# Mixing over the sequence on column quarters and row quarters of the PE array

## The chip, the cores and the metric

The kernel runs on one core of a Trainium2 chip. Its time is device microseconds (us) of one execution; lower is better. Three executions of the kernel before were timed, and a fourth was recorded by the hardware profiler. The engines are PE (matrix multiply, with PEld for its weight loads), DVE (vector), ACT (scalar), POOL (GpSimd) and SP, which issues the DMAs.

## What is computed

The inputs are q, k and v for 4 batches of 8 heads, 576 tokens, 64 wide, all float32, and the matrices U (576 x 32), V (32 x 576), w_ch1 (512 x 2048) and w_ch2 (2048 x 512), which arrive as 64-bit floats.

```python
q_rot, k_rot = (rotate(q), rotate(k))            # rotary embedding
scores = scale * np.matmul(q_rot, k_rot.transpose(0, 1, 3, 2))
scores = scores - np.max(scores, axis=-1, keepdims=True)
attn = np.exp(scores)
attn = attn / (np.sum(attn, axis=-1, keepdims=True) + 1e-09)
x = np.matmul(attn, v)                           # then as (batch, 576, 512)
h = x.transpose(0, 2, 1) @ U @ V                 # the mix over the sequence
u = x + h.transpose(0, 2, 1)
ch = np.maximum(u @ w_ch1, 0.0) @ w_ch2
out = u + ch
```

## The kernel before

**Stages.** Attention of a batch runs over four head pairs (`hp`, 128 features each) and, within a pair, over five token tiles (`t`): four of 128 tokens and a rest of 64 (`REM`). A tile's scores go into the PSUM buffers `s`, DVE finds the maximum (`junk`, `nb`), ACT takes the exponential (`p`), ACT and POOL split it into two f16 halves, and SP turns them by a transposing DMA (`pt<-p`). PE multiplies by V in f16 parts (`pv`), the result is divided by the row sums into `xf` (tokens on partitions), and PE turns that against an identity (`ident`) into `x` (features on partitions). The scores of batches 0 and 1 are f32 matmuls of 64 rows, two heads on the two row halves of the array; batches 2 and 3 use three f16 matmuls instead.

**The mix** (`mix`, line 1123) follows each second head pair, so twice a batch. `project` multiplies `uf` by the five `xf` tiles of two pairs: 5 f32 matmuls of 256 columns into one PSUM bank. `uf` (filled in `prep_uv`, line 643) holds U three times side by side and a fourth block of zeros, so 96 of the 128 result rows carry the same product. `parts` copies them into `gt` as f32r, a reduced-precision 4-byte type, and DVE writes what was rounded off into rows 32 to 63. `spread` then multiplies `gt` by `vst` (V three times, one copy holding V's own rounding rest): per chunk of 128 features 2 f32r matmuls of 288 columns. DVE adds the result to `x` and takes the largest magnitude, `am`.

**Scales.** `pow2_scale` and `half_scales` add a per-partition sum over the 128 partitions by a matmul with an all-ones matrix (`ones`, f32, 1 or 2 columns) and make a power of two of it. This happens 21 times in all: once per batch for V and for u (4 + 4), for the five weight groups, and for eight head pairs of batches 2 and 3.

**The MLP** works on 8 halves (batch, 288 tokens). The first half of batch 0 is plain f32 (`mm<-x,wt` and an f32 form of `mm<-room,wt`, 256 matmul records); the other seven take three f16 matmuls of 288 columns per product (`mm<-u,wt`, `mm<-room,wt`, 2,688 records). Attention of batch b+1 is interleaved with the MLP of batch b. A half can start when `ready[b]` has the scale of u, which needs the whole mix of its batch.

**What sets the order.** The class `Plan` records every step with its engine and its reads and writes, gives each a cost (`cost`, `transfer`, `lag`), places them as early as their engine and inputs allow, and orders each engine by the start times. Then each row of `MOVES` (52 of them: a seed, a spread, a begin and a width) shakes a stretch of that order; the shortest by the planner's own costs is kept and emitted. The engines' queues follow it strictly. All instructions therefore carry line 379 in the profile, and are told apart by their tiles.

Of the kernel before, what the change touches and what calls it, by code (L numbers as in the profile page):

```python
# [59 lines left out]
class Plan:  # L60
# [85 lines left out]
    @staticmethod  # L146
    def cost(calls):

        us = 0
        for eng, op, a, k in calls:  # L150
            out = k.get("out", a[0] if a else None)
            ins = [k[i] for i in ("in_", "in0", "in1") if i in k]
            n = max(free(x) for x in [out] + ins)
            by = sum(hasattr(k.get(i), "tensor") for i in ("scale", "scalar", "scalar1", "scalar2"))
            psum = any(x.space == PSUM for x in ins)
            if eng == "tensor":
                m = free(a[1] if op == "transpose" else a[2])
                if op == "transpose":
                    us += free(a[0]) / 1200
                    if "xf" in a[1].tensor.name:  # L160
                        us += 0.05 if free(a[0]) > 64 else 0.12
                elif a[2].dtype == F32:

                    k = 2 if list(a[1].ap)[0][1] <= 64 and m > 256 and len(calls) == 4 else 1
                    us += max(m * 4, 640 if free(a[1]) > 1 and m > 1 else 256) / 2400 / k
                    us += 0.05 * (k > 1)
                else:
                    k = 2 if list(a[1].ap)[0][1] <= 64 and len(calls) == 12 else 1
                    us += max(m, 64) * (4 if a[2].dtype == F32R and m < 256 else 1) / 2400 / k
                us += 0.003  # L170
            elif eng == "vector":
                fast = op in ("tensor_scalar", "tensor_copy") and not psum
                us += n * (0.00052 if fast else 0.00104)
                us += 0.008 if op == "memset" else 0.069 + 0.062 * by
            elif eng == "scalar":
                by += "accum_out" in k
                by += hasattr(k.get("bias"), "tensor")
                us += n * 0.00083 + (0.053 if psum else 0.094) + 0.093 * by
            elif op == "memset":
                us += 0.035 + n * 0.00083  # L180
            elif op == "tensor_tensor":
                us += 0.148 + n * (0.0021 if k["in1"].dtype in (F32, F32R) else 0.00189)
            else:
                us += 0.161 + 0.083 * by + n * 0.00083
        eng, op, a, k = calls[0]
        if eng == "tensor" and op == "matmul":
            if list(a[1].ap)[0][1] <= 64 and len(calls) in (4, 12):
                us += 0.18 if len(calls) == 12 else 0.06
            elif len(calls) == 5 and free(a[2]) == 256:
                us += 0.3  # L190
            elif a[2].dtype == F32R:
                us += 0.07
            elif free(a[2]) <= 2:
                us += 0.12
        return us
# [36 lines left out]
    def transfer(calls):  # L232
# [3 lines left out]
        if op == "dma_start_transpose":  # L236
            return 1.37, 0.9, 1.3, 0.98
# [3 lines left out]
        return hw, hw + 0.65, rows * free(sb) * SIZE[sb.dtype] / 360e3, 1.2  # L241
# [36 lines left out]
    def lag(a, b, turn=False):  # L278

        if a == "sync":  # L280
            return 0.98 if turn else 1.2
# [121 lines left out]
def tile_rope_attention_then_mixer(ctx, tc, qk, v, tab, u_in, v_in, w1, w2, out):  # L403
# [54 lines left out]
    ones = cst.tile([P, P], F32, name="ones")  # L458
# [30 lines left out]
    vst = cst.tile([P, S], F32R, name="vst")  # L489

    uf = cst.tile([P, NC, 4 * R], F32, name="uf")
    xfs = [cst.tile([P, 2, P], F32, name=f"xf{t}") for t in range(NC)]
# [32 lines left out]
    gt = cst.tile([P, DM], F32R, name="gt")  # L525
# [58 lines left out]

    def pow2_scale(sq, nm, up):
# [3 lines left out]
        nc.tensor.matmul(pb[:, 0:1], ones, sq, start=True, stop=True)  # L589
# [53 lines left out]
    def prep_uv():  # L643
# [10 lines left out]
        room = u.rearrange("p a c s -> p (a c s)").bitcast(F32)  # L654
        vr = room[:, 0:S]
        ur = room[:, S:S + NC * R].rearrange("p (c r) -> p c r", r=R)
        single((ur[:, 0:NT], ud[:, 0:NT]), (ur[0:REM, NT], ud[0:REM, NT]), (vr, vd))
        fill(uf[:, :, 3 * R:4 * R], 0.0)
        for n, cc in ((P, slice(0, NT)), (REM, slice(NT, NC))):
            for i in range(3):  # L660
                copy(uf[:n, cc, i * R:(i + 1) * R], ur[:n, cc, :], "ADP")
        copy(vst, vr, "ADP")
        lo = slice(2 * R, 3 * R)
        two(vst[lo, :], vr[lo, :], vst[lo, :].bitcast(F32), ALU.subtract, "DP")


# [222 lines left out]
    def half_scales(b, hp):  # L889
# [8 lines left out]
        nc.tensor.matmul(pb[:, 0:2], ones, sq, start=True, stop=True)  # L898
# [149 lines left out]
    def values(b, hp, t, pts, sm):  # L1048
# [25 lines left out]
        def evac():  # L1074
# [10 lines left out]
            xt = xfs[t][:, hp % 2]  # L1085
# [19 lines left out]
        def turn():  # L1105
# [7 lines left out]
            nc.tensor.transpose(tp[:, 0:n], xt[0:n], ident[0:n, 0:n])  # L1113
# [6 lines left out]
        if hp % 2 and t == NT:  # L1120
            mix(b, hp // 2)

    def mix(b, i):

        x, am = state[b]["x"], state[b]["am"]
        hold = {}

        beside = b == 0 and i < BES

        def project():  # L1130
            hold["t1"] = bank("") if beside else scores(1)[:, 0]
            with nc.group():
                for t in range(NC):
                    n = P if t < NT else REM
                    nc.tensor.matmul(
                        hold["t1"][:, 0:256], uf[:n, t, :],
                        xfs[t][:n].rearrange("p c d -> p (c d)"),
                        start=(t == 0), stop=(t == NT),
                    )

        def parts():
            g = gt[:, i * 256:(i + 1) * 256]
            t1 = hold["t1"]
            copy(g, t1[:, 0:256], "AD")
            lo = slice(R, 2 * R)
            nc.vector.tensor_tensor(
                out=g[lo, :], in0=t1[lo, 0:256], in1=g[lo, :].bitcast(F32), op=ALU.subtract
            )

        def spread(c):  # L1150
            xc = x[:, c, :].rearrange("p (n s) -> p n s", n=2)
            ph = None if beside else scores(1)
            for n in range(2):
                o = bank("") if beside else ph[:, n]
                nc.tensor.matmul(
                    o[:, 0:HS], gt[:, c * P:(c + 1) * P], vst[:, n * HS:(n + 1) * HS],
                    start=True, stop=True,
                )
                if beside:
                    nc.vector.tensor_tensor(  # L1160
                        out=xc[:, n], in0=o[:, 0:HS], in1=xc[:, n], op=ALU.add
                    )
            if not beside:
                nc.vector.tensor_tensor(out=xc, in0=ph[:, :, 0:HS], in1=xc, op=ALU.add)
            nc.vector.tensor_reduce(
                out=am[:, c:c + 1], in_=x[:, c, :], axis=AX.X, op=ALU.max,
# [3 lines left out]
        def last():  # L1170
            am1 = tmp("amu1", [1], 2, f"amu1{b}")
            nc.vector.tensor_reduce(out=am1, in_=am, axis=AX.X, op=ALU.max)
            sq = tmp("squ", [1], 2, f"squ{b}")
            nc.vector.tensor_tensor(out=sq, in0=am1, in1=am1, op=ALU.mult)


            ready[b] = (x, *pow2_scale(sq, f"u{b}", 4))

        project()
        parts()  # L1180
        spread(2 * i)
        spread(2 * i + 1)
        if i == NP // 2 - 1:
            last()
# [7 lines left out]
    def open_batch(b):  # L1192
        state[b].update(
            am=tmp("amu", [NP], 2, f"amu{b}"),
# [306 lines left out]
```

## Time and profile before

| | us |
|---|---|
| three timed executions | 678.32, 679.35, 679.36 (median 679.35) |
| the profiled execution, span from first to last instruction | 671.3 |
| what lies around the span (median less span) | 8.05 |
| PE busy / DVE / ACT / POOL, of the span | 620.9 / 437.1 / 388.1 / 239.1 |

The profiled execution's time is its span and the 8.05 us around it. A PE record is one pass: an f32 matmul has two records. Matmuls are pipelined, so the duration of one record is longer than its share of PE's time; what a row of matmuls costs is read from its start to the start of the next row.

### The profile page before, as it was taken

To read this page: it belongs to the slowest core of one execution; us is meant where nothing else is said; L and a number is where in the kernel's file an instruction comes from. 1 tells how busy PE (TensorE), PEld (TensorE's weight loads), DVE (VectorE), ACT (ScalarE), POOL (GpSimd) and SP (SyncE) were. 2 spreads that over 40 slices of the span, in tenths; PEclk is the share of its full clock that TensorE was granted. 3 is DMA by queue.
4 is the path that set the end of the run, shared out by engine and by line. 5 is a ranking of instruction groups with operands and counts; after the bars stand their busy time and mean duration, and the time that the engine had idled before them with its cause. 6 is when DMAs were issued, how large, how long until landed. Compare 5 with 4: busy or idle time off the path is not lost.

```text
span 671.3 us, 15150 instructions
## 1 busy us (share of the span) xinstructions
PE 620.9 (92%) x5914; PEld 467.9 (70%) x5914; DVE 437.1 (65%) x1096; ACT 388.1 (58%) x794; POOL 239.1 (36%) x205
## 2 busy tenths in 40 slices
PE   2677887999998999999999999999999999999998
PEld 1445555777776677777777777777777777777776
DVE  4678887999877866767767775667768643430310
ACT  3647775576877687467765874468766661320210
POOL 1456653013366567033454543044433450000000
PEclk9978888999999999999999999999999999999999
DMA  8899999979968657346786768168564561000000
GB/s 245 177 262 226 233 213 277 354 227 214 185 125 178 139 96 124 105 129 127 144 140 132 141 116 159 40 155 174 106 132 84 102 118 46 19 1 27 10 10 27
DMA packets 198056, 92.57 MB, mean 138 GB/s; under 512 B 173280, under 2 KB 186592, under 8 KB 197984
## 3 DMA queue, kind: packets, MB, share of 16 engines
q1 hardware_dynamic: 197984, 91.61, 61.6%
q8 instruction: 46, 0.75, 0.5%
q14 instruction: 26, 0.21, 0.1%
HBM read 41.70 MB, written 4.72 MB: 69 GB/s over the span
## 4 chain that ended last, share of the span: by engine, by line
PE 50%; DMA 7%; DVE 3%; issue 2%; ACT 2%; POOL 2%; SPq 0%; ACTq 0%; POOLq 0%; DVEq 0%
PE mm L379 38%; PE s L379 7%; DMA pt<-p 5%; PE pv L379 5%; DMA raw<-qk 1%; ACT p L379 1%; POOL p L379 1%; DVE junk L379 1%; DVE room L379 0%; DVE raw L379 0%; DVE u L379 0%; POOL raw L379 0%; ACT room L379 0%; SPq L379 0%; DVE x L379 0%
## 5 line engine op out<-in xcount | busy, mean ns | idle before, releaser
L379 PEld LDWEIGHTS <-wt 128*128 128x128 f16 x2688 | 255.0, 98 | 73.4 <-issue 13.2
L379 POOL TENSOR_TENSOR p<-p,p 128x576 f16<-128x576 f32 x130 | 171.6, 1328 | 209.3 <-ACT p L379 144.7
L379 PE MATMUL mm<-room,wt 128*128 128x288 f16 (+1 forms) x1472 | 219.6, 297 | 0.0
L379 PE MATMUL mm<-u,wt 128*128 128x288 f16 x1344 | 183.6, 286 | 1.7 <-DVE room L379 1.4
L379 ACT ACTIVATE room<-mm 128x288 f16<-128x288 f32 (+1 forms) x128 | 52.0, 408 | 97.1 <-PE mm L379 90.1
L379 PE MATMUL s<-qk,qk 64*128 64x288 f16 (+1 forms) x640 | 84.7, 371 | 18.8 <-DVE qk L379 11.2
L379 PEld LDWEIGHTS <-pt 128*128 128x128 f16 x1918 | 79.0, 100 | 29.6 <-DMA pt<-p 16.6
L379 DVE SCALAR_TENSOR_TENSOR room<-mm,room 128x288 f16<-128x288 f32 x112 | 50.9, 456 | 67.8 <-ACT room L379 67.2
L379 ACT ACTIVATE p<-p 128x576 f16<-128x576 f32 x130 | 86.9, 681 | 12.1 <-DMA pt<-p 10.6
L379 DVE TENSOR_SCALAR_CACHE_REDUCE junk<-s,bqk 128x576 bf16<-128x576 f32 x72 | 58.1, 812 | 22.7 <-PE s L379 18.6
L379 ACT ACTIVATE p<-s,nb,bqk 128x576 f32<-128x576 f32 x72 | 59.0, 828 | 21.6 <-DVE nb L379 14.9
L379 ACT ACTIVATE p<-s,nb 128x576 f32<-128x576 f32 x72 | 51.9, 737 | 26.0 <-DVE junk L379 20.3
L379 DVE TENSOR_SCALAR_CACHE_REDUCE junk<-s 128x576 bf16<-128x576 f32 x72 | 52.6, 753 | 18.4 <-PE s L379 16.6
L379 PE MATMUL pv<-vh,pt 128*128 128x65 f16 (+1 forms) x600 | 57.4, 200 | 6.7 <-DMA pt<-p 5.6
L379 PE MATMUL pv<-vl,pt 128*128 128x64 f16 (+1 forms) x600 | 57.2, 200 | 0.3 <-DVE vl L379 0.3
L379 PEld LDWEIGHTS s<-qk,qk 64*128 64x128 f32 x256 | 30.2, 216 | 33.0 <-ACT p L379 13.0
L379 DVE SCALAR_TENSOR_TENSOR ob<-mm,so,x 128x288 f32<-128x288 f32 x28 | 14.4, 514 | 41.3 <-PE mm L379 41.2
L379 ACT ACTIVATE xf<-pv,rc 128x64 f32<-128x64 f32 (+1 forms) x95 | 25.7, 309 | 25.6 <-DVE rc L379 23.0
L379 PE MATMUL pv<-vb,pt 128*128 128x65 f16 (+1 forms) x480 | 36.5, 200 | 1.1 <-DMA vb<-vh 1.1
L379 PE MATMUL mm<-x,wt 128*128 128x288 f32 x128 | 33.9, 420 | 1.7 <-DVE x L379 1.6
L379 DVE TENSOR_SCALAR rs<-pv,sc_v 128x2 f32<-128x2 f32 x67 | 14.5, 217 | 29.8 <-PE pv L379 28.5
L379 ACT ACTIVATE x<-mm 128x128 f32<-128x128 f32 (+1 forms) x59 | 15.5, 263 | 30.7 <-PE mm L379 30.5
(148 smaller groups left out, 714.9 us busy)
## 6 DMA issues: line engine op xcount, KB each, us to landing
raw<-qk SPq DMA_DIRECT2D x30, 576.0 KB, 4.6
wt<-w SPq DMA_DIRECT2D x23, 512.0 KB, 5.8
out_t<-ob SPq DMA_DIRECT2D x32, 144.0 KB, 2.0
raw<-vt SPq DMA_DIRECT2D x8, 512.0 KB, 4.8
x<-w SPq DMA_DIRECT2D x6, 512.0 KB, 5.5
vb<-vh SPq DMA_DIRECT2D x8, 264.0 KB, 4.9
pt<-p SPq DMA_TRANSPOSE x130, 3.3
u<-w SPq DMA_DIRECT2D x3, 512.0 KB, 5.4
```

The source lines that it names most:

```text
L379: getattr(getattr(nc, eng), op)(*a, **k)
```

## The change

Three things are altered in the computation.

- **Mix.** `uf` holds U once (32 columns) in f32 and `vst` holds V four times, unsplit. Per token tile and chunk one f32 matmul of 128 columns gives 32 result rows; chunk c writes to partitions 32c to 32c+31 of one bank, so the four chunks use the four column quarters of the array. The copy into `gt` is f32 and has no rounding rest. The spread takes chunk c from rows 32c to 32c+31: f32 matmuls of 32 rows and 288 columns on four row quarters, into four PSUM banks. Batch 0 still mixes after each second pair, on two quarters; batches 1 to 3 mix once, after the last pair, and there the spread goes in two rounds, one for each half of the sequence, which reuse the two `s` buffers.
- **Last token tile.** Rows 64 to 127 of its `xf` and `uf` are zero, so its turn and its projection use all 128 rows.
- **Scales.** `ones` and the summed column are bf16 (the upper half of each f32), one pass instead of two.

Several of the planner's costs are altered, and `MOVES` has 169 rows instead of 52, all with other numbers; the whole order is made anew.

```diff
 MOVES = (
-    (2201, 0.3, -489, 100), (7090, 0.3, -200, 40), (3748, 0.3, -65, 10), (365, 0.3, -230, 10),
...
+    (8915, 3, -514, 40), (390, 0.3, -332, 20), (5639, 0.3, -292, 40), (9035, 0.3, -270, 100),
...
-    ones = cst.tile([P, P], F32, name="ones")
+    ones = cst.tile([P, P], BF16, name="ones")
...
-    vst = cst.tile([P, S], F32R, name="vst")
-    uf = cst.tile([P, NC, 4 * R], F32, name="uf")
-    xfs = [cst.tile([P, 2, P], F32, name=f"xf{t}") for t in range(NC)]
+    vst = cst.tile([P, S], F32, name="vst")
+    uf = cst.tile([P, NC, R], F32, name="uf")
+    xfs = [cst.tile([P, NP, P], F32, name=f"xf{t}") for t in range(NC)]
...
+    def upper(sq):
+        return sq.bitcast(BF16)[:, 1::2]
...
-        nc.tensor.matmul(pb[:, 0:1], ones, sq, start=True, stop=True)
+        nc.tensor.matmul(pb[:, 0:1], ones, upper(sq), start=True, stop=True)
...
-        fill(uf[:, :, 3 * R:4 * R], 0.0)
-        for n, cc in ((P, slice(0, NT)), (REM, slice(NT, NC))):
-            for i in range(3):
-                copy(uf[:n, cc, i * R:(i + 1) * R], ur[:n, cc, :], "ADP")
-        copy(vst, vr, "ADP")
-        lo = slice(2 * R, 3 * R)
-        two(vst[lo, :], vr[lo, :], vst[lo, :].bitcast(F32), ALU.subtract, "DP")
+        fill(uf[REM:P, NT, :], 0.0)
+        fill(xfs[NT][REM:P], 0.0)
+        single((uf[:, 0:NT], ud[:, 0:NT]), (uf[0:REM, NT], ud[0:REM, NT]), (vst, vd))
...
-            nc.tensor.transpose(tp[:, 0:n], xt[0:n], ident[0:n, 0:n])
+            nc.tensor.transpose(tp[:, 0:P], xt, ident)
...
-                    nc.tensor.matmul(
-                        hold["t1"][:, 0:256], uf[:n, t, :],
-                        xfs[t][:n].rearrange("p c d -> p (c d)"),
-                        start=(t == 0), stop=(t == NT),
+                for c in cc:
+                    nc.tensor.matmul(
+                        t1[own[c]], uf[:, t], xfs[t][:, c], start=t == 0, stop=t == NT
                     )
...
+        def spread(ways):
+            with nc.group():
+                for o, c, n in ways:
+                    nc.tensor.matmul(
+                        o[:, 0:HS], gt[own[c]], vst[own[c], n * HS:(n + 1) * HS],
+                        start=True, stop=True,
+                    )
+
+        if len(cc) == NP:
+            for n in range(2):
+                hs = slice(n * HS, (n + 1) * HS)
+                ph = [scores(b) for _ in range(NP // 2)]
+                spread([(ph[c // 2][:, c % 2], c, n) for c in cc])
+                for i, p in enumerate(ph):
+                    xc = x[:, 2 * i:2 * i + 2, hs]
+                    nc.vector.tensor_tensor(out=xc, in0=p[:, :, 0:HS], in1=xc, op=ALU.add)
+                    largest(2 * i, 2, hs, 2 * n + 4 * i)
```

The order shows the mix of batch 1 on PE. Before, the second of its two projections (`xf_85` to `xf_89` are the five token tiles, `uf` is U, `s_62` the result, `wt` the MLP's weights) stands among MLP matmuls:

```order
L379 LDWEIGHTS wt
L379 MATMUL mm_65<-u,wt 128x288
L379 MATMUL s_62<-xf_85,uf 128x256
L379 MATMUL s_62<-xf_86,uf 128x256
L379 MATMUL s_62<-xf_87,uf 128x256
L379 MATMUL s_62<-xf_88,uf 128x256
L379 MATMUL s_62<-xf_89,uf 128x256
```

The one projection of batch 1 after the change, with its neighbours on PE:

```order
L414 LDWEIGHTS wt
L414 MATMUL mm_64<-room,wt 128x288
L414 MATMUL mm_66<-xf_85,uf 32x128 x4
L414 MATMUL mm_66<-xf_86,uf 32x128 x4
L414 MATMUL mm_66<-xf_87,uf 32x128 x4
L414 MATMUL mm_66<-xf_88,uf 32x128 x4
L414 MATMUL mm_66<-xf_89,uf 32x128 x4
```

Two rows of five matmuls with 256 columns became one row of twenty with 128 columns and 32 result rows, and the result moved from an `s` buffer to a bank.

On DVE, the end of batch 1's mix before (`gt` is the projection, `x_72` the activations, `amu` the largest magnitudes, `squ` the input of the scale of u):

```order
L379 TENSOR_TENSOR raw_100<-raw_100 128x576
L379 TENSOR_TENSOR gt<-s_61,gt 32x256
L379 TENSOR_TENSOR x_72<-s_61,x_72 128x576
L379 TENSOR_TENSOR x_72<-s_62,x_72 128x576
L379 TENSOR_REDUCE amu<-x_72 128x1 x2
L379 TENSOR_REDUCE amv_130<-amv 128x1
L379 TENSOR_REDUCE amu_136<-amu 128x1
L379 TENSOR_TENSOR squ<-amu_136 128x1
```

and the same place on DVE after the change:

```order
L414 TENSOR_TENSOR raw_100<-raw_100 128x576
L414 TENSOR_TENSOR x_72<-s_61,x_72 128x2x288
L414 TENSOR_TENSOR x_72<-s_62,x_72 128x2x288
L414 TENSOR_REDUCE amu<-x_72 128x2 x2
L414 TENSOR_REDUCE amv_130<-amv 128x1
L414 TENSOR_TENSOR x_72<-s_62,x_72 128x2x288
L414 TENSOR_TENSOR x_72<-s_61,x_72 128x2x288
L414 TENSOR_REDUCE amu<-x_72 128x2 x2
L414 TENSOR_REDUCE amu_136<-amu 128x1
L414 TENSOR_TENSOR squ<-amu_136 128x1
```

The subtraction for `gt` is gone, and the adds and reductions of the first two chunks, which stood some eighty instructions earlier, now stand at the batch's end with the others. On PE 15 MLP matmuls stand between the two rounds of this spread, and 30 between its last matmul and the sum for `squ` in batch 3; 21 MLP matmuls of batch 2 follow that sum, before and after the change.

On SP, the DMA issues of batch 0's third head pair before (`wt<-w` loads 512 KB of MLP weights):

```order
L379 DMA_TRANSPOSE pt<-p_2_98 128x9x128
L379 DMA wt<-w 128x2x512
L379 DMA_TRANSPOSE pt<-room 128x9x128
L379 DMA_TRANSPOSE room<-room 128x9x128
L379 DMA_TRANSPOSE pt<-p_0_96 128x9x128
```

and, after the change, the longest row of such loads on SP in batch 0:

```order
L414 DMA_TRANSPOSE pt<-room 128x9x128
L414 DMA_TRANSPOSE room<-room 128x9x128
L414 DMA wt<-w 128x2x512 x6
L414 DMA_TRANSPOSE pt<-p_0_96 128x9x128
L414 DMA_TRANSPOSE pt<-p_1_97 128x9x128
```

Loads that stood one or two at a time between the transposes stand six in a row, and about as many have been issued by the end of that stretch.

## Rows read from the trace of the kernel before

**Rows 1.** The page's span, and its busy time of the engines.
```profile
span 671.3 us, 15150 instructions
...
PE 620.9 (92%) x5914; PEld 467.9 (70%) x5914; DVE 437.1 (65%) x1096; ACT 388.1 (58%) x794; POOL 239.1 (36%) x205
```

**Rows 2.** Busy time by stretch; columns as in the first line.
```profile
core 0: us, PE busy (x) PEld busy (x) DVE busy (x) ACT busy (x) POOL busy (x), PEclk, DMA share, GB/s
0.00:50.00 50.00, 26.96 (x171) 16.62 (x172) 32.66 (x79) 25.65 (x42) 18.45 (x24) 0.91 0.93 228
...
109.00:120.00 11.00, 8.17 (x46) 5.34 (x43) 10.47 (x22) 4.19 (x15) 1.71 (x2) 1.00 1.04 391
...
120.00:671.30 551.30, 538.53 (x5200) 412.31 (x5200) 346.27 (x875) 314.28 (x642) 182.76 (x152) 1.00 0.54 116
```

**Rows 3.** What PE waited for before 120 us: total, times, longest.
```profile
PE s L379 <- DVE qk L379: 11.2, 1, 11.2
PE s L379 <- ACT p L379: 8.9, 9, 4.3
```

**Rows 4.** Timeline of PE, batch 1: start, duration, operation, count. Projection and turns.
```profile
214.81 0.27 PE L379 MATMUL mm<-ident,xf 128*128 128x128 f32 x1
214.92 0.65 PE L379 MATMUL mm<-u,wt 128*128 128x288 f16 x4
215.41 2.52 PE L379 MATMUL s<-xf,uf 128*128 128x256 f32 x10
217.85 0.54 PE L379 MATMUL mm<-u,wt 128*128 128x288 f16 x3
218.33 0.27 PE L379 MATMUL mm<-ident,xf 64*128 64x64 f32 x1
218.53 0.66 PE L379 MATMUL mm<-u,wt 128*128 128x288 f16 x4
```

**Rows 5.** Timeline of PE, the spread of the same mix and what follows.
```profile
220.59 0.80 PE L379 MATMUL s<-vst,gt 128*128 128x288 f32 x4 [0.78 <-DVE gt L379]
221.23 0.79 PE L379 MATMUL mm<-u,wt 128*128 128x288 f16 x5
221.85 0.19 PE L379 MATMUL pv<-vh,pt 128*128 128x65 f16 x1
221.88 0.20 PE L379 MATMUL pv<-vl,pt 128*128 128x64 f16 x1
```

**Rows 6.** Timeline of PE, f32 scores on two row halves.
```profile
161.06 1.24 PE L379 MATMUL s<-qk,qk 64*128 64x288 f32 x8
162.23 0.99 PE L379 MATMUL mm<-room,wt 128*128 128x288 f32 x3
```

**Rows 7.** Timeline of PE, sums for scales and their neighbours, at two places.
```profile
192.42 0.41 PE L379 MATMUL mm<-room,wt 128*128 128x288 f32 x1
192.66 0.28 PE L379 MATMUL mm<-smw,ones 128*128 128x1 f32 x2
192.80 0.53 PE L379 MATMUL mm<-u,wt 128*128 128x288 f16 x3
...
246.60 0.28 PE L379 MATMUL mm<-sqk,ones 128*128 128x2 f32 x2
246.92 0.23 PE L379 MATMUL pv<-vh,pt 128*128 128x130 f16 x1
```

**Rows 8.** Timeline of DVE in batch 0's second mix.
```profile
114.60 0.42 DVE L379 TENSOR_TENSOR gt<-s,gt 32x256 fp32r<-32x256 f32 x1
...
116.44 0.76 DVE L379 TENSOR_TENSOR x<-s,x 128x576 f32<-128x576 f32 x1
117.23 0.75 DVE L379 TENSOR_REDUCE amu<-x 128x1 f32<-128x576 f32 x1
```

**Rows 9.** The projection's weight loads by tile: minimum, median, maximum ns.
```profile
L379 PEld LDWEIGHTS s<-xf,uf x70: 183/190/248, 110.3 to 563.7; 128*128 128x128 f32 x56, 64*128 64x128 f32 x14
```

More of the change, by code (lines that the diff above doesn't have):

```diff
@@ L155, in cost @@
             psum = any(x.space == PSUM for x in ins)
-            if eng == "tensor":
+            if eng == "tensor" and op == "matmul" and list(a[1].ap)[0][1] == 32:
+                us += free(a[2]) / 600 / (4 if len(calls) == 4 and calls[2][2][1] is not a[1] else 2)
+            elif eng == "tensor" and op == "matmul" and free(a[1]) == 32:
+                us += free(a[2]) / 600 / (len(calls) // 5)
+            elif eng == "tensor":
                 m = free(a[1] if op == "transpose" else a[2])
@@ L160, in cost @@
                     if "xf" in a[1].tensor.name:
-                        us += 0.05 if free(a[0]) > 64 else 0.12
+                        us += 0.02
                 elif a[2].dtype == F32:
@@ L172, in cost @@
                 fast = op in ("tensor_scalar", "tensor_copy") and not psum
+                if fast and out.dtype == I32 and n >= 256:
+                    us += n * 0.00027
                 us += n * (0.00052 if fast else 0.00104)
@@ L188, in cost @@
                 us += 0.18 if len(calls) == 12 else 0.06
-            elif len(calls) == 5 and free(a[2]) == 256:
-                us += 0.3
+            elif free(a[1]) == 32 or list(a[1].ap)[0][1] == 32:
+                us += 0.25
             elif a[2].dtype == F32R:
@@ L193, in cost @@
             elif free(a[2]) <= 2:
-                us += 0.12
+                us += 0.0
         return us
@@ L236, in transfer @@
         if op == "dma_start_transpose":
-            return 1.37, 0.9, 1.3, 0.98
+            return 1.37, 0.9, 1.5, 0.8
         sb = out if out.space != bass.MemoryType.DRAM else in_
@@ L240, in transfer @@
         hw = 0.45 if rows == 128 else 0.62
-        return hw, hw + 0.65, rows * free(sb) * SIZE[sb.dtype] / 360e3, 1.2
+        return hw, hw + 0.65, rows * free(sb) * SIZE[sb.dtype] / 335e3, 1.1
     def place(self, n):
@@ L280, in lag @@
         if a == "sync":
-            return 0.98 if turn else 1.2
+            return 0.8 if turn else 1.1
         if a == b:
@@ L524, in tile_rope_attention_then_mixer @@
     raw_ring = cycle([cst.tile([P, NC * DM // 2], F32, name=f"raw{i}") for i in range(3)])
-    gt = cst.tile([P, DM], F32R, name="gt")
+    gt = cst.tile([P, P], F32, name="gt")
     u = cst.tile([P, 2, NP, HS], F16, name="u")
@@ L653, in prep_uv @@
             nc.sync.dma_start(vd[i * R:(i + 1) * R].rearrange("p s t -> p (s t)"), v_in)
[L654 to L657, printed above, removed]
-        fill(uf[:, :, 3 * R:4 * R], 0.0)
-        for n, cc in ((P, slice(0, NT)), (REM, slice(NT, NC))):
-            for i in range(3):
-                copy(uf[:n, cc, i * R:(i + 1) * R], ur[:n, cc, :], "ADP")
-        copy(vst, vr, "ADP")
-        lo = slice(2 * R, 3 * R)
-        two(vst[lo, :], vr[lo, :], vst[lo, :].bitcast(F32), ALU.subtract, "DP")
+        fill(uf[REM:P, NT, :], 0.0)
+        fill(xfs[NT][REM:P], 0.0)
+        single((uf[:, 0:NT], ud[:, 0:NT]), (uf[0:REM, NT], ud[0:REM, NT]), (vst, vd))
     iw = cst.tile([P, NP], F32, name="iw")
@@ L897, in half_scales @@
         pb = bank("")
-        nc.tensor.matmul(pb[:, 0:2], ones, sq, start=True, stop=True)
+        nc.tensor.matmul(pb[:, 0:2], ones, upper(sq), start=True, stop=True)
         a = tmp("aqk", [2], 2, "")
@@ L1084, in evac @@
             nc.vector.reciprocal(out=rc, in_=rs)
-            xt = xfs[t][:, hp % 2]
+            xt = xfs[t][:, hp]
             hold["xt"] = xt
@@ L1119, in values @@
         turn()
-        if hp % 2 and t == NT:
-            mix(b, hp // 2)
-    def mix(b, i):
-        x, am = state[b]["x"], state[b]["am"]
[L1126 to L1134, printed above, removed]
+        if t == NT:
+            if b == 0 and hp % 2:
+                mix(b, (hp - 1, hp))
+            elif hp == NP - 1:
+                mix(b, range(NP))
@@ L1135, in project, with mix @@
+    def mix(b, cc):
+        x, am = state[b]["x"], state[b]["am"]
+        cc = list(cc)
+        own = [slice(c * R, (c + 1) * R) for c in range(NP)]
+        rows = slice(own[cc[0]].start, own[cc[-1]].stop)
+        t1 = bank("")[:, 0:P]
+        with nc.group():
+            for t in range(NC):
+                for c in cc:
                     nc.tensor.matmul(
-                        hold["t1"][:, 0:256], uf[:n, t, :],
-                        xfs[t][:n].rearrange("p c d -> p (c d)"),
-                        start=(t == 0), stop=(t == NT),
-                    )
@@ L1141, in parts @@
[L1141 to L1154, printed above, removed]
-                nc.tensor.matmul(
[L1156 to L1164, printed above, removed]
+                        t1[own[c]], uf[:, t], xfs[t][:, c], start=t == 0, stop=t == NT
+                    )
@@ L1165, in spread, with largest @@
+        copy(gt[rows], t1[rows], "AD")
+        def largest(c, k, hs, o):
             nc.vector.tensor_reduce(
-                out=am[:, c:c + 1], in_=x[:, c, :], axis=AX.X, op=ALU.max,
+                out=am[:, o:o + k], in_=x[:, c:c + k, hs], axis=AX.X, op=ALU.max,
                 apply_absolute_value=True,
             )
[L1170 to L1184, printed above, removed]
+        def spread(ways):
+            with nc.group():
+                for o, c, n in ways:
[12 more added lines that the diff above has]
+                    largest(2 * i, 2, hs, 2 * n + 4 * i)
+        else:
+            ph = [scores(b) for _ in cc]
+            spread([(p[:, n], c, n) for n in range(2) for p, c in zip(ph, cc)])
+            for p, c in zip(ph, cc):
+                xc = x[:, c].rearrange("p (n s) -> p n s", n=2)
+                nc.vector.tensor_tensor(out=xc, in0=p[:, :, 0:HS], in1=xc, op=ALU.add)
+                nc.vector.tensor_reduce(
+                    out=am[:, 2 * c:2 * c + 2], in_=xc, axis=AX.X, op=ALU.max,
+                    apply_absolute_value=True,
+                )
@@ L1186, in begin @@
+        if cc[-1] < NP - 1:
+            return
+        am1 = tmp("amu1", [1], 2, f"amu1{b}")
+        nc.vector.tensor_reduce(out=am1, in_=am, axis=AX.X, op=ALU.max)
+        sq = tmp("squ", [1], 2, f"squ{b}")
+        nc.vector.tensor_tensor(out=sq, in0=am1, in1=am1, op=ALU.mult)
+        ready[b] = (x, *pow2_scale(sq, f"u{b}", 4))
     def begin(b, hp):
@@ L1193, in open_batch @@
         state[b].update(
-            am=tmp("amu", [NP], 2, f"amu{b}"),
+            am=tmp("amu", [2 * NP], 2, f"amu{b}"),
             x=xs_[b % 2],
```

55 rows, old and new, of the table MOVES are left out of this document.

## Prediction

> **What bounds the kernel now.** First the busy times: PE works 620.9 of 671.3 us, the next engine, DVE, 437.1 [rows 1]. Then the stretches, since a share over the span mixes two regimes. In the first 50 us PE is busy for 26.96 us; from 120 us to the end it is busy for 538.53 of 551.3, and only 12.8 us are left in which it stands idle [rows 2]. What PE waits for before 120 us is the chain of batch 0's attention: 11.2 us until the first q and k are ready, and 8.9 us in nine waits for ACT's exponentials [rows 3]. So after 120 us a microsecond of PE's work is worth nearly one of time, and before it only what shortens the chain counts. I read PE's work from start to start in the timeline, as durations overlap. An f16 matmul of 288 columns takes 0.122 us (four of them from 214.92 to 215.41), an f32 pass of 128 columns 0.11 (214.81 to 214.92) [rows 4], and an f32 pass of 288 columns 0.24 (192.42 to 192.66) [rows 7].
>
> **The projection.** One takes 2.44 us, from 215.41 to 217.85 [rows 4]. Batches 1 to 3 have six after 120 us: 14.6 us. After the change each has one, of 20 matmuls in two passes of 128 columns: 40 passes at 0.11 are 4.4 us one after another and 1.1 us if four quarters run together. Column quarters do not occur in the trace. The nearest rows are the scores on two row halves: 8 passes from 161.06 to 162.23, 1.17 us [rows 6], where 8 single passes at 0.24 would be 1.92; four pairs are 0.96, so they overlap fully, and 0.21 us more go with the change of shape on entering and leaving. I take full overlap from those rows: 1.1 + 0.2 = 1.3 us, three times 3.9. Saved: 10.7 us. The other end is no overlap, 4.6 us each, 13.8 in all, 0.8 saved.
>
> **The spread.** Four f32r matmuls take 0.64 us, from 220.59 to 221.23 [rows 5]; six of these are 3.8 us. After the change a round has 4 matmuls, 8 passes of 0.24: 0.48 us on four row quarters, and 0.2 for the shape. Six rounds make 4.1 us: 0.3 lost. Here the row halves of [rows 6] are the same mode, with two in place of four. One after another a batch's 16 passes would take 3.84 + 0.4 = 4.2 us, 12.7 in all, 8.9 lost.
>
> **The last tile's turn.** From 217.85 to 218.53 lie three MLP matmuls (0.37) and one turn of 64 rows: 0.31 us, where one of 128 rows takes 0.11 [rows 4]. The padded tile should cost as the others do: 0.2 saved, 12 times after 120 us, 2.4 us. Should the excess not go, nothing is saved. The zeros are written once, at the start, where PE waits for the first q and k anyway.
>
> **The sums for scales.** One costs PE between 0.14 us (192.66 to 192.80) and 0.32 (246.60 to 246.92) [rows 7]. In bf16 it is one pass; the nearest row is an f16 matmul of 65 columns, 0.03 us (221.85 to 221.88) [rows 5]. So 0.11 to 0.29 saved, 20 of the 21 after 120 us: 2.2 to 5.8. I take 2.2, since most sums stand among MLP matmuls, as the one at 192.66.
>
> **Start.** Batch 0's second mix lies on the chain that lets the MLP begin. Its projection of 2.4 us becomes 20 passes on two quarters, 1.1 + 0.2; the subtraction of 0.42 us on DVE [rows 8] goes; the spread of 0.64 becomes 4 x 0.24 + 0.2 = 1.2. Together 1.0 us gained. DVE and ACT also lose five copies and a subtraction for U and V; other work of that stretch hides them, so nothing is counted.
>
> **What the mix adds at a batch's end.** Before, DVE had there the subtraction, two adds and two reductions, 0.42 + 2 x 0.76 + 2 x 0.75 = 3.4 us; now four and four, 6.0 us [rows 8]. Behind them in DVE's queue stand the scale of u and the splits that the next MLP half needs. In the order 15 MLP matmuls (1.8 us) stand between the rounds and 21 (2.6 us) after the sum, and they cover it. The second round must wait until DVE has emptied both `s` buffers, 1.5 us of adds, and all of PE's queue waits behind it: cover 1.8 us, tight if DVE is still at an earlier step. I charge 1.0 us for the three batches; without cover it would be 3 x 2.6 = 7.8.
>
> **The sum.** After 120 us -10.7 + 0.3 - 2.4 - 2.2 = -15.0; start -1.0; waits +1.0; together -15.0. The span goes from 671.3 to 656.3, and the 8.05 us around it stay: 664.4, or 664 us, beside a median of 679.35. The remade order I count at zero: it moves waits, which this trace prices only by their total.
>
> **Rivals.**
>
> *Weight loads of the column quarters are not hidden.* The projection's weight loads take 0.19 us for 128 columns [rows 9], and all lie beside passes of 0.24 us (2.44 us for ten) [rows 4]. A quarter's load of 32 columns I estimate at a quarter of it, 0.047; bared, 40 of them add 1.9 us to a projection, 5.7 us in all: 670.1. For it: the quarters share the array's rows, and a pass of 128 columns hides half of what one of 256 does. Against it: on the row halves the loads of one half lie beside the passes of the other. Much the same time comes out if the quarters run two and two: projections 2.4 (+3.3), rounds 1.2 (+2.9), 670.6.
> The Trainium skill (TensorE: Matmul & The Clock Gate, Part 3: Packing small matmuls — row/col tiling) states that a weight load overlaps a running matmul only if its row group differs, which column quarters do not offer. By that rule this rival comes true, at its 670.1; the present projection speaks against it, as its loads overlap passes on the same rows [rows 9]. The page also gives measured speedups of 3.07 for four row tiles and 2.38 for three column tiles; by 3.07 in place of 4 in both steps I estimate from it some 2 us less gain, 666.
>
> *The quarters run one after another, and the kernel gets slower.* The projection saves 0.8 in place of 10.7 (+9.9), the spread loses 8.9 in place of 0.3 (+8.6), and batch 0's mix takes 2.4 and 2.1 us in place of 1.3 and 1.2 (+2.0): 684.9. For it: no row shows quarters. Against it: the halves overlap fully [rows 6]. The point from which it decides: the 24.7 us of passes (3 x (4.4 + 3.84)) shrink to 6.2 at full overlap; where overlap shortens them by a factor under about 1.2, to 21 us, the 15 us are used up.
>
> *Batch 0 starts later.* SP now has six 512 KB loads in a row ahead of the transposes that feed PE, before at most two there. At the 391 GB/s of the stretch with most loads [rows 2] one takes 1.34 us; four more in front make 5.4 us: 669.8. For it: DMA was 0.93 busy in the first 50 us [rows 2]. Against it: the loads were due soon in any case, and the transposes of the pairs before now go unhindered.
>
> *The new order closes idle time as well.* If half of the 12.8 us after 120 us [rows 2] and of the 8.9 us before [rows 3] goes: 10.8 us less, 653.6. For it: waits are small and many, which an order can mend. Against it: an order follows the planner's costs, not the chip's.
>
> **Chances and range.** The forecast 0.48; weight loads bared, or two and two 0.17; later start 0.13; better order 0.11; one after another 0.08; several of the losses together, so that nothing is left, 0.03. The range reaches from 654, at the better order, to 673, above either of the two small losses with some of the other; outside lie the slower case, the null and part of the better order, under 0.2. A measurement of this kernel tells about 0.2% from no change: faster by more 0.89, within it 0.03, slower 0.08.
>
> **What would show it.** Right: the projection of batches 1 to 3 takes 1.2 to 1.4 us from start to start, a round of the spread 0.6 to 0.8, the last turn as much as the others; PE's busy time after the MLP's begin falls by 14 to 16 us while its idle stays near 13. Wrong: a projection above 3 us; PE idle at the second round for DVE; the adds of batch 0's second mix later than 116.4 us [rows 8]; or, with all steps right, an idle share that swallows or doubles the gain, which would be the order's doing.

## The result, and the profile after

The kernel after takes 659.75 us (median of four executions, 659.09 to 661.54); the kernel before took 678.84 beside it (four, 676.98 to 679.36). The ratio is 0.9734, with a 95% interval of 0.9711 to 0.9757. The profiled execution took 659.51 us.

The page of the kernel after, span and busy times, as in [rows 1]:

```profile
span 657.8 us, 15277 instructions
...
PE 603.7 (92%) x6005; PEld 456.5 (69%) x6005; DVE 438.3 (67%) x1094; ACT 386.5 (59%) x783; POOL 224.1 (34%) x196
```

PE has 17.2 us less to do, with 91 more records; DVE and ACT are within 2 us of where they were, and POOL has 15.0 us less. By stretch, with the columns of [rows 2]:

```profile
0.00:50.00 50.00, 28.50 (x214) 19.13 (x215) 35.12 (x86) 29.92 (x51) 23.20 (x24) 0.93 0.97 219
109.00:120.00 11.00, 9.20 (x81) 6.40 (x81) 7.90 (x18) 6.33 (x20) 0.00 (x0) 0.80 1.01 309
120.00:657.80 537.80, 523.68 (x5272) 401.80 (x5272) 353.45 (x885) 311.67 (x628) 169.60 (x147) 1.00 0.58 122
```

After 120 us PE is idle for 14.1 us, before for 12.8 [rows 2]. So the gain is work that PE no longer has, not idle time closed. What PE still waits for from 120 us on (total, times, longest):

```profile
PE pv L414 <- DMA pt<-p: 7.1, 12, 1.2
PE mm L414 <- DVE room L414: 1.5, 3, 0.6
PE mm L414 <- DVE x L414: 0.9, 1, 0.9
```

The mix of batch 1 on PE (start, duration, operation, count), where [rows 4] and [rows 5] showed the old one:

```profile
274.01 0.65 PE L414 MATMUL mm<-room,wt 128*128 128x288 f16 x4
274.59 1.30 PE L414 MATMUL mm<-xf,uf 128*32 128x128 f32 x40
275.82 0.79 PE L414 MATMUL mm<-room,wt 128*128 128x288 f16 x5
276.54 0.77 PE L414 MATMUL s<-vst,gt 32*128 32x288 f32 x8
277.24 2.01 PE L414 MATMUL mm<-room,wt 128*128 128x288 f16 x15
279.18 0.77 PE L414 MATMUL s<-vst,gt 32*128 32x288 f32 x8
279.88 3.97 PE L414 MATMUL mm<-room,wt 128*128 128x288 f16 x31
283.69 0.17 PE L414 MATMUL mm<-squ,ones 128*128 128x1 bf16 x1
283.72 0.53 PE L414 MATMUL mm<-room,wt 128*128 128x288 f16 x3
```

From start to start the projection takes 1.23 us (274.59 to 275.82), a round of the spread 0.70, and the sum 0.03. No bracket stands behind any of these rows: PE waits for nothing here.

**How the runs below are compared.** In every profile there is one row in which PE takes up the f32 MLP after a wait for DVE's first add into `x`, in batch 0's second mix. From before (a second profile) and from after:

```profile
120.58 1.24 PE L379 MATMUL mm<-x,wt 128*128 128x288 f32 x4 [1.38 <-DVE x L379]
```
```profile
120.31 10.06 PE L414 MATMUL mm<-x,wt 128*128 128x288 f32 x39 [0.91 <-DVE x L414]
```

From there to the end of the span I call the *stretch*; what lies ahead of it is the *start*. The stretch repeats well: 554.05 and 554.22 us in two profiles of the kernel before, 537.49 and 536.76 in two of the kernel after. The start does not: 117.3 and 120.6 before, 120.3 and 124.1 after, and 119.1 to 127.2 in all profiles that have the new order. So single profiles are compared by their stretch, and medians carry the scatter of the start. Each stretch of an edited kernel rests on one profile.

### The profile page after: what moved, and what is told of

The parts are those of the page before. It is cut to its first block, busy times and chain, and to the rows that moved or that the text cites. A ratio compares the mean times of both kernels' runs of the same rounds, so it can differ in the third digit from the quotient of the medians.

```text
span 657.8 us, 15277 instructions
## 1 busy us (share of the span) xinstructions
PE 603.7 (92%) x6005; PEld 456.5 (69%) x6005; DVE 438.3 (67%) x1094; ACT 386.5 (59%) x783; POOL 224.1 (34%) x196
## 4 chain that ended last, share of the span: by engine, by line
PE 66%; DMA 12%; DVE 10%; ACT 7%; issue 3%; POOL 2%; SPq 1%; POOLq 0%; ACTq 0%; DVEq 0%
PE mm L414 50%; PE s L414 11%; DMA pt<-p 8%; PE pv L414 6%; ACT p L414 4%; DVE wt L414 3%; DVE junk L414 3%; DMA raw<-qk 2%; POOL p L414 1%; DVE raw L414 1%; ACT room L414 1%; ACT xf L414 1%; DMA vb<-vh 1%; DMA cs<-tab 1%; SPq L414 1%
## 5 line engine op out<-in xcount | busy, mean ns | idle before, releaser
L414 POOL TENSOR_TENSOR p<-p,p 128x576 f16<-128x576 f32 x130 | 173.6, 1342 | 179.2 <-ACT p L414 139.5
L414 PE MATMUL mm<-room,wt 128*128 128x288 f16 (+1 forms) x1472 | 217.0, 297 | 0.0
L414 PE MATMUL s<-qk,qk 64*128 64x288 f16 (+1 forms) x640 | 82.4, 372 | 18.7 <-DVE qk L414 11.5
L414 ACT ACTIVATE p<-p 128x576 f16<-128x576 f32 x130 | 87.2, 681 | 12.8 <-DMA pt<-p 11.2
L414 ACT ACTIVATE p<-s,nb,bqk 128x576 f32<-128x576 f32 x72 | 59.1, 829 | 24.8 <-DVE nb L414 13.8
L414 PEld LDWEIGHTS s<-qk,qk 64*128 64x128 f32 x256 | 30.2, 219 | 32.8 <-ACT p L414 14.4
L414 DVE SCALAR_TENSOR_TENSOR ob<-mm,so,x 128x288 f32<-128x288 f32 x28 | 14.4, 515 | 43.6 <-PE mm L414 43.0
L414 ACT ACTIVATE xf<-pv,rc 128x64 f32<-128x64 f32 (+1 forms) x92 | 24.8, 309 | 19.2 <-DVE rc L414 15.6
L414 DVE SCALAR_TENSOR_TENSOR wt<-wt 128x512 int32<-128x512 int32 x46 | 31.8, 722 | 0.1
```

Source lines behind the costliest of these rows:

```text
L414: getattr(getattr(nc, eng), op)(*a, **k)
```

## The experiments

Except where the text says otherwise, the new order is kept instruction for instruction, so that a run differs from the kernel after by its edit alone. The diffs are shortened to the line that counts, written as it would stand in the kernel; in the runs the altered instructions were put in after the order was fixed. PE busy and idle are those of the stretch, from one row of busy times each; 537.1 us, the mean of two, stands for the kernel after. Three expectations (small_undone, spread_serial, all_undone) count otherwise, from batch 0's second mix to the last unbroken row of matmuls, 514.2 us in the kernel after; there 517.5, 524.3 and 533.0 were measured. That of sums_four counts to the last matmul: 533.5, and 550.8 measured.

| run | median us | ratio to before, 95% | stretch | PE busy | PE idle |
|---|---|---|---|---|---|
| before (recorded, again) | 678.27 | 1.0011 (0.9993 to 1.0029) | 554.05, 554.22 | 541.00, 542.22 | 13.1, 12.0 |
| after (recorded, again) | 659.75, 661.23 | 0.9734, 0.9744 | 537.49, 536.76 | 523.68, 523.71 | 13.8, 13.1 |
| project_serial | 666.89 | 0.9845 (0.9823 to 0.9867) | 545.21 | 530.79 | 14.4 |
| spread_serial | 670.70 | 0.9909 (0.9881 to 0.9936) | 546.70 | 533.56 | 13.1 |
| turn_64 | 660.93 | 0.9746 (0.9725 to 0.9766) | 539.72 | 525.73 | 14.0 |
| sums_f32 | 659.90 | 0.9745 (0.9717 to 0.9773) | 535.57 | 525.70 | 9.9 |
| small_undone | 663.36 | 0.9802 (0.9775 to 0.9829) | 540.43 | 528.16 | 12.3 |
| sums_four | 678.25 | 1.0007 (0.9991 to 1.0022) | 554.41 | 539.99 | 14.4 |
| all_undone | 680.21 | 1.0038 (1.0019 to 1.0058) | 554.75 | 543.05 | 11.7 |
| loads_spread | 665.47 | 0.9825 (0.9783 to 0.9866) | 536.69 | 523.28 | 13.4 |
| before_no_moves | 692.56 | 1.0220 (1.0193 to 1.0248) | 567.00 | 546.20 | 20.8 |
| after_no_moves | 681.01 | 1.0033 (1.0002 to 1.0064) | 560.95 | 536.10 | 24.9 |

### Both kernels a second time

> The changed kernel once more, unaltered, as the reference for the runs beside it. Both theories expect 659 to 662 us.

> The kernel before, unaltered, for a second profile of it. Theory 'the recorded start was short': the first profile's span (671.3) was some 6 us below what its median stands for, so this one has a span of 675 to 678 and the projection of batch 0's second mix starts at 114 to 118 us, not 110.5. Rival 'the new order starts later': it starts near 110.5 again, and the changed kernel, at 116 to 120, loses about 6 us there.

The kernel after: 661.23 us (657.86 to 662.60), a ratio of 0.9744 (0.9718 to 0.9770). The kernel before: 678.27, a span of 674.8 in an execution of 676.57, its second mix of batch 0 at 113.8 us, where the recorded one had it at 110.5; both are 0.2 us short of the bounds given (675 and 114), but it does not start near 110.5 again, as the rival had it. Where time and span of one execution are known, 1.7 to 1.8 us lie around the span. The 8.05 us of the prediction were not that: the recorded execution was an early one, whose MLP began some 5 us ahead of the typical start, which the median gives as 678.3 - 1.7 - 554.1 = 122.5 us. By the same sum the kernel after starts at 121 to 122.4. The start has not changed, then, within what these runs can tell.

### The projection without overlap

```diff
-for t in range(NC):
-    for c in cc:
+for c in cc:
+    for t in range(NC):
         matmul(t1[own[c]], uf[:, t], xfs[t][:, c], start=t == 0, stop=t == NT)
```

> The changed kernel, every instruction in its place, but the twenty matmuls of a projection stand chunk by chunk instead of tile by tile, so that five in a row use the same column quarter and cannot run beside each other. Theory 'PE's passes' (after batch 0 a microsecond of PE work is a microsecond of time): a projection of batches 1 to 3 grows from 1.3 to about 4.6 us, +9.9 us, batch 0 adds 1 to 2: 670 to 672. Theory 'order' (the gain comes from the remade order, and PE's work hides in waits): under 662.

PE's timeline in this run, at the same place:

```profile
276.83 3.34 PE L415 MATMUL mm<-xf,uf 128*32 128x128 f32 x40
280.10 0.79 PE L415 MATMUL mm<-room,wt 128*128 128x288 f16 x5
```

A projection takes 3.27 us. That is less than 4.6, since at each of the three changes of chunk four passes still run beside four of the next (12 x 0.109 = 1.3 us). Three projections cost 3 x 2.04 = 6.1 us more, the stretch is 8.1 longer, and the median 6 to 7. The missed size is that of the edit; what PE spends here comes back in time in full, with 2 us more. Measured from the stretch's beginning, the three projections start 0.0, 2.9 and 5.7 us later than in the recorded profile of after, so what goes beyond 6.1 us grows between the mixes, in two steps of 0.8. The two profiles of after differ by 1.4 us at the second of them (292.3 and 290.9 us), so the 2 us are not shown to be the edit's.

Ahead of all three projections the granted clock also falls to its lower level for a while, after PE waited 0.93 us for `p`; the kernel after waits 0.79 us at that place and keeps the full clock. PEclk is the third number from the end:

```profile
176.90:180.30 3.40, 3.40 (x10) 1.97 (x9) 2.23 (x9) 2.07 (x6) 1.28 (x1) 0.51 1.29 180
```

The profiles of spread_serial and sums_four have a like fall near there (0.50, from 175.9 and 177.7 us). Yet the first projection starts 154.2 us into the stretch here (276.83 - 122.59), in the two profiles of after 154.3 and 153.4: by then the loss is within their scatter. From 60 to 140 us of the stretch, within batch 1's attention, PE idles 3.5 us here, 5.0 and 3.8 there. So there is one place in the stretch whose waits can take a loss of PE's up.

### The spread without overlap

```diff
-matmul(o[:, 0:HS], gt[own[c]], vst[own[c], n * HS:(n + 1) * HS])
+matmul(o[:, 0:HS], gt[own[cc[0]]], vst[own[cc[0]], n * HS:(n + 1) * HS])
```

> The order of the kernel after is kept, but every spread matmul takes the row quarter of the first chunk of its mix, so that none can run beside another (the result is that of one chunk, four times). A round of eight passes at 0.24 us and 0.2 for the shape should then take 2.1 us in place of 0.70: +1.4 for each of six rounds and +0.9 for batch 0, 9.3 us in all. If PE's work sets the end there: stretch 523 to 524, median 669 to 671. If waits of the attention at a batch's end absorb it: below 664. If quarters of the rows do not run beside one another in the kernel after, nothing changes and the round stays at 0.70.

The timeline of PE in it:

```profile
278.62 2.20 PE L415 MATMUL s<-vst,gt 32*128 32x288 f32 x8
280.76 2.01 PE L415 MATMUL mm<-room,wt 128*128 128x288 f16 x15
```

A round takes 2.14 us in place of 0.70. Six make 8.6 us; the stretch is 9.6 longer and the median about 10. The overlap of four row quarters is real, and its loss comes back in full. (Here and in all_undone the spread leaves the result of one chunk four times; the runs are for the time alone.)

### The last turn on 64 rows, and the sums in f32

```diff
-transpose(tp[:, 0:P], xt, ident)
+transpose(tp[:, 0:n], xt[0:n], ident[0:n, 0:n])
```
```diff
-matmul(pb[:, 0:1], ones, upper(sq), start=True, stop=True)
+matmul(pb[:, 0:1], ones32, sq, start=True, stop=True)
```

> The changed kernel in its own order, with the last token tile turned on 64 rows again (16 turns); the projection keeps 128 rows. 'PE's passes': 0.2 us for each of 12 turns after the start, +2.4 us, 662 to 663, and each such turn followed by a gap in the trace. Rival: the turn's change of shape hides in waits, under 661.

> The changed kernel in its own order, with the 21 sums for scales in f32 again, two passes with wide weight loads. 'PE's passes': +2.2 to +2.8 us, 662 to 663. 'Order': under 661.

> The order of the kernel after is kept, and both small savings are undone together: sums in f32 with two passes, last tile's turn on 64 rows. The two runs apart showed no longer time, while PE's work grew by 2.3 us in each. If these 4.6 us were only hidden by the start, which differs between executions by some 4 us, the stretch from batch 0's second mix to the last matmul grows from 514.2 (514.5 and 513.8 in two profiles) to 518 or 519, and the median is near 665. If waits take them up, the stretch stays at 513 to 516 and the median at 660 to 662.

Neither median moved: 660.93 and 659.90. The stretch tells them apart. With the old turn it is 2.6 us longer, as the timeline of that run lets one expect:

```profile
271.02 0.78 PE L415 MATMUL mm<-room,wt 128*128 128x288 f16 x5
271.73 0.27 PE L415 MATMUL mm<-ident,xf 64*128 64x64 f32 x1
271.94 0.66 PE L415 MATMUL mm<-room,wt 128*128 128x288 f16 x4
```

The turn takes 0.21 us, and the five matmuls ahead of it 0.71 in place of 0.61: 0.31 together, 0.20 more than the 0.11 of a full one, twelve times. The median does not show it: the start was early, 119.1 us in that profile, the earliest with the new order, and 660.9 - 1.7 - 539.7 = 119.5 by the median. Why it was early is not shown. With f32 sums PE is 2.0 us busier, but the stretch is 1.5 us shorter and the idle time falls to 9.9. Both together make the stretch 3.3 us longer and the median 2 to 4. So the turn counts. The sums alone do not, and that is no chance of one profile. Busy times from 60 to 140 us of the stretch, after and with f32 sums:

```profile
180.31:260.31 80.00, 75.01 (x797) 55.35 (x796) 65.21 (x161) 66.96 (x132) 37.79 (x30) 1.00 0.76 147
```
```profile
182.53:262.53 80.00, 78.17 (x839) 58.11 (x838) 67.29 (x167) 69.71 (x134) 39.94 (x31) 1.00 0.72 151
```

PE idles 5.0 us in the one and 1.8 in the other. In all four profiles with f32 sums it is 1.8 to 2.0, in the six others of the new order (loads_spread with them) 3.5 to 5.0. So some 2 us of waits in batch 1's attention go when the sums take longer; why they go, no run shows.

### The sums made large

```diff
-matmul(pb[:, 0:1], ones, upper(sq), start=True, stop=True)
+for _ in range(4):
+    matmul(pb[:, 0:1], ones32, sq, start=True, stop=True)
```

> Order of the kernel after; each sum for a scale is the f32 matmul of two passes, and is issued four times over (the result is the same each time), so that what a sum costs is made large. In the run with f32 sums the 20 sums took 3.2 us of PE's time in place of 1.0 to 1.3, and the stretch from the ninth MLP matmul to the last matmul did not grow (531.9 beside 533.9 and 533.1). Three further issues at 0.16 us make 9.8 us more, about 12 in all over the kernel after. If PE's time counts there one to one, as the prediction took it, the stretch goes to 543 to 546 and the median to 670 to 673. If the sums lie in front of waits that take them up, the stretch stays below 538 and the median below 665.

The sum for the scale of u of batch 0, in PE's timeline:

```profile
140.97 0.95 PE L415 MATMUL mm<-squ,ones 128*128 128x1 f32 x8
141.78 2.19 PE L415 MATMUL mm<-x,wt 128*128 128x288 f32 x8
```

One sum of eight passes costs 0.81 us in place of 0.03, twenty of them 15.6. That is more than I expected (0.64), so the bounds I gave are missed on the far side; the stretch is 17.3 us longer and the median 17 to 18.5. At this size the sums come back in full; at one f32 sum each, 2 us in all, they did not.

### All four undone in the new order

The four edits above together, with sums of two passes.

> Order of the kernel after; projection chunk by chunk, spread on one row quarter (the result is that of one chunk, four times), sums in f32 and the last turn on 64 rows, all together. The single runs give +8.4 us of the stretch for the projection, 9.3 expected for the spread, 4.6 of work for the two small ones. If they add up: stretch 535 to 537, median 681 to 683, slower than the kernel before by some 3 us, and the gain of the change is all in what the quarters and the passes save. If waits absorb the small ones or the sum: median 674 to 679.

Busy times of its stretch, and of that of the kernel before (second profile):

```profile
127.25:682.00 554.75, 543.05 (x5292) 417.05 (x5292) 354.30 (x884) 311.09 (x628) 170.92 (x147) 1.00 0.56 117
```
```profile
120.58:674.80 554.22, 542.22 (x5208) 414.72 (x5208) 349.43 (x880) 314.69 (x643) 183.98 (x154) 1.00 0.54 118
```

The stretch is 17.6 us longer than that of the kernel after, where the single runs sum to 8.1 + 9.6 + 3.3 = 21.0. The median lies between the two that were expected. Where the 3.4 us went stays open; what the two serial runs took beyond PE's own work, 2.0 and 1.0 us, would be most of it. It equals the stretch of the kernel before, but its parts do not: the projections are shorter than before's (3.3 against 2 x 2.44 a batch) and the rounds longer. With about the same work for PE, the old and the new order leave the same idle time, 11.7 against 12 to 13 us. So the new order as such is worth nothing that shows here, and a loss of the size of the gain comes of the four edits.

### The order without its search

```diff
-MOVES = (... 52 rows before, 169 after ...)
+MOVES = ()
```

> The kernel before with an empty table MOVES: the planner's first order, not shaken. Theory 'PE's passes': slower than before by what the search had given, and the changed kernel with an empty table is 14 to 19 us faster than this one, as with the tables. Rival 'order': the two without tables are less than 9 us apart, the rest of the gain being the longer search's.

> The changed kernel with an empty table MOVES, against the kernel before with an empty table. 'PE's passes': 14 to 19 us below it. 'Order': less than 9 us below it.

Without the rows of `MOVES` the change is worth 692.56 - 681.01 = 11.6 us, with them 17 to 19: between the two theories. In the stretch it is 6.0 against 17.0; the other 5.6 lie in the start. Both unsearched orders leave more idle time, and that of the changed kernel more (24.9 against 20.8). From 200 to 240 us alone it idles 8.4 us where the other idles 2.6. Busy times by stretch without the search, first after, then before:

```profile
200.00:220.00 20.00, 13.24 (x118) 8.59 (x116) 15.90 (x34) 13.83 (x23) 8.22 (x6) 0.83 0.76 142
220.00:240.00 20.00, 18.35 (x189) 13.87 (x190) 12.85 (x42) 15.38 (x36) 11.68 (x8) 0.83 0.77 137
```
```profile
200.00:220.00 20.00, 17.52 (x186) 12.54 (x182) 15.12 (x43) 16.02 (x35) 12.40 (x10) 1.00 0.73 120
220.00:240.00 20.00, 19.92 (x192) 14.73 (x193) 15.25 (x40) 15.75 (x30) 16.24 (x11) 1.00 0.51 123
```

In these 40 us PE works 31.6 us where the other works 37.4, and after its idle spells the granted clock is 0.83 on average, so that what it does there is slower too. In the whole stretch PE is busy for 14.3 us at a granted clock of 0.50 (in 176.2 to 179.5, 203.5 to 210.3 and 220.5 to 227.3 us), in that of the other kernel for 6.0; if half of that is lost, an estimate, the clock costs 7.1 and 3.0 us. With the idle time these are 7 to 8 of the 11 us by which the unsearched pair falls short. Which of the altered steps makes the unsearched order bad there was not tried.

### The six loads in a row

Of the six `wt<-w` loads in a row, two stay together and the other four are moved behind transposes: two stand behind a `pt<-p`, one behind a `pt<-room`, one behind a `room<-room`. The rest of the order stays.

> The changed kernel in its own order, only that five of the six weight loads that stand in a row on SP in batch 0 are moved behind the transposes that follow, one or two at a time. 'The new order starts later' because the loads stand ahead of the transposes: batch 0's second mix starts 3 to 5 us earlier, 655 to 658. Rival (loads do not hold the start up): 659 to 662.

665.47 us, about 5 more than the kernel after. The stretch is the same (536.69), so all of the loss lies in the start: 665.47 - 1.7 - 536.7 = 127 us. The start did not come earlier, as it should if the row held it up; with the loads pulled apart it came later. Which wait grew is not settled: PE waits for `p` 11.6 us in this start, but 12.1 us in that of the second profile of after.

## Why the prediction was right, and where its terms were off

The forecast was 15.0 us less, 664 us, inside a range of 654 to 673; the runs give 17 to 19 less, 660 to 661 us. Step by step:

- **What bounds it: right.** After 120 us PE's work is the time. Work put back came back as time in every run in which it was large: 6.1 us as 8.1, 8.6 as 9.6, 15.6 as 17.3. The exception is batch 1's attention, whose waits took up 2 us with the f32 sums.
- **The projection, -10.7: right.** Full overlap and a price for the change of shape were taken from the scores on row halves [rows 6]: 1.3 us. It is 1.23, so 6 x 2.44 - 3 x 1.23 = 10.9 us are saved.
- **The spread, +0.3: the round right, the present cost wrong.** A round is 0.70 us where 0.68 was worked out. But the old cost was taken from one group of four in a row, 0.64 us [rows 5], and five of the six groups were issued in pieces. The next one in the trace of before:

```profile
279.52 0.39 PE L379 MATMUL s<-vst,gt 128*128 128x288 f32 x1
279.84 0.27 PE L379 MATMUL mm<-ident,xf 64*128 64x64 f32 x1
280.04 0.54 PE L379 MATMUL s<-vst,gt 128*128 128x288 f32 x2
280.42 0.66 PE L379 MATMUL mm<-room,wt 128*128 128x288 f16 x4
280.83 0.39 PE L379 MATMUL s<-vst,gt 128*128 128x288 f32 x1
281.06 1.15 PE L379 MATMUL mm<-room,wt 128*128 128x288 f16 x8
```

  From start to start these are 0.32 + 0.38 + 0.23 = 0.93 us. All six come to 5.4 us, not 3.8. In four of them a piece stands just ahead of a turn of 64 rows and takes 0.32 us in place of 0.23; these 0.09 are in the turn's price already. Without them it is 5.0 us, and the step is -0.8.
- **The last turn, -2.4: right**, by its undoing (+2.6 in the stretch of one profile).
- **The sums, -2.2: too small by the rows, and not shown as time.** In a row of MLP matmuls 0.14 us became 0.03. Counted one by one and without idle time, the twenty fell from 3.7 us to 0.8, since half of those before stood at dearer places; that is -2.9. Undone alone they made the stretch 1.5 us shorter; only four times as large did they count.
- **Waits at a batch's end, +1.0: not there.** The cover that was called tight held. DVE's timeline:

```profile
277.34 1.42 DVE L414 TENSOR_TENSOR x<-s,x 128x576 f32<-128x576 f32 x2
278.68 1.40 DVE L414 TENSOR_REDUCE amu<-x 128x2 f32<-128x576 f32 x2
280.06 1.41 DVE L414 TENSOR_TENSOR x<-s,x 128x576 f32<-128x576 f32 x2
```

  The adds that empty the `s` buffers end at 278.76 us, and PE comes to the second round at 279.18, from its 15 MLP matmuls. In batches 2 and 3 PE comes to it without a wait as well.
- **The start, -1.0: not seen**, within a scatter of 3 to 4 us. The sign of being wrong that the prediction set here did come: the adds of batch 0's second mix start at 119.5 and 123.3 us, later than 116.4. It was a bad sign, taken from an early execution; in the second profile of before they start at 119.8.
- **The 8.05 us around the span: wrong**, 1.7 us. It did no harm, because the difference was set against the median in the end.
- **The remade order at zero: right** for the two orders as they are, and that is luck: no row of the prediction priced it, and without the searches the gain in the stretch is 11 us smaller.

Terms of PE's work: -10.9 - 0.8 - 2.4 - 2.9 = -17.0, where its busy time in the stretch fell by 17.3 (541.0 to 523.7) and the stretch by 17.0. The 3 us more than forecast there (-14.0) are the spread's 1.1, the wait's 1.0, the sums' 0.7 and the projection's 0.2. That the parts meet the whole to some tenths is luck: the undoings, which are the test in time, do not add up so closely.

Of the rivals, *weight loads not hidden* fell by the loads' own row (minimum, median, maximum ns) and the projection's time:

```profile
L414 PEld LDWEIGHTS mm<-xf,uf x160: 106/110/178, 64.0 to 549.4; 128*32 128x32 f32 x160
```

Forty loads of 110 ns lie beside forty passes in 1.23 us, and four passes run at once. The estimate of 47 ns for a load was less than half of that, and still nothing is bared. The Trainium skill (TensorE: Matmul & The Clock Gate, Part 3: Packing small matmuls — row/col tiling) would have a load overlap only if its row group differs; column quarters share all their rows, and this trace disagrees with that rule. *Two and two* fell with it. *One after another* fell by the two serial runs. *Later start* has the least against it: by the medians the start did not move (121 to 122.4 us, before 122.5), in two profiles of each kernel it is 3 us later, and loads_spread did not bring it forward. *Better order* fell by the idle time of the stretch, 12.0 and 13.1 us before, 13.1 and 13.8 after.

## What to carry to other kernels

Where one engine is busy to within 3%, count its work from start to start, and count every group: one group of six is no price for the others. Where small products use a part of the array, issue them so that neighbours in the queue lie on different quarters; here the order of two loops made 2 us of a 3.3 us step. Before a start is compared, look at how it scatters: a piece of the program that repeats to within 1 us shows a 2.6 us effect that the medians hid. And look for waits that can take a small change up: here they lay in the attention of one batch.

## What the chip showed that was not expected

- Four f32 matmuls on four column quarters start 6 to 7 ns apart, and each next four 109 ns after the four before, the second four 134 (40 passes from 274.59 to 275.82 us); on four row quarters 7 ns apart as well. Entering and leaving the shape costs 0.1 us each: from the MLP matmul ahead to the first quarter 216 ns, where two MLP matmuls are 122 apart, and 205 ns behind the last, where a pass is 109.
- With the new order the granted clock is lower in the start: 0.85 and 0.83 on average over the first 124 us, before 0.90 and 0.88. Before, it falls most from 30 to 60 us (0.79 and 0.73), after, from 60 to 90 (0.62 and 0.61). From 60 to 90 us, first before (second profile), then after:

```profile
60.00:90.00 30.00, 22.53 (x248) 16.09 (x245) 21.32 (x59) 20.64 (x42) 17.05 (x15) 0.93 1.02 204
```
```profile
60.00:90.00 30.00, 23.05 (x170) 15.40 (x172) 20.73 (x46) 15.63 (x33) 13.69 (x12) 0.62 0.98 235
```

  PE is busy for about as long in both, in the second with fewer matmuls (170 for 248), and is granted 0.93 in the one and 0.62 in the other. A mean of 0.62 says that it stood at the lower of its two levels (1.2 and 2.4 GHz) for most of these 30 us. By the medians the MLP began no later for it.
- The start differed by up to 8 us between profiles of the new order (119.1 to 127.2, the edits in it small), while the stretch behind it repeated to within 1 us for the same kernel.
